# Rows 4 and 5 of a Fourier mix: their own products in place of mirrored reads of the products of rows 1 and 2

## The chip, the cores and the metric

The kernel runs on one core of one Trainium2 chip. A core has TensorE (PE) for matrix products, VectorE (DVE), ScalarE (ACT) and GpSimd (POOL) for elementwise work, and SyncE (SP), which here only issues transfers. ACT and POOL issue transfers as well, in line with their other instructions. Each engine works through its own list in order, and semaphores order the engines against each other and against the 16 DMA engines. The metric is device time of one execution in microseconds (us), as the median of three runs; the profile is of one further recorded look at one execution, with its own time.

## The reference

The input is q, k, v of shape (4 batches, 8 heads, 768 positions, 64). First comes attention with ALiBi slopes, in which a position sees the 96 latest positions and the first 8; then a Fourier mix and a two-layer product with a residual:

```
x = attention(q, k, v)                       # per batch 768 x 512
X = np.fft.fft(np.fft.fft(x, axis=1), axis=2)
u = x + np.real(X)
un = (u - mean(u)) / sqrt(var(u) + 1e-6)     # over the 512 columns
out = u + relu(un @ w_ch1) @ w_ch2           # 512 x 2048, 2048 x 512
```

The real part of a 2-D transform of real numbers is symmetric: its value at (position s, column d) is the value at (768 - s, 512 - d), both taken modulo the size.

## The kernel before

**Tiling.** A position is written as s = 6m + r, with m from 0 to 127 on the partitions and r from 0 to 5, the "row" of the title. A column is d = 4n + rd. The transform is split so that a short sum over tiles is made on VectorE and the rest are matmuls. Each batch b passes through these steps: loads and casts of q, k, v (`load`, L353; `cast_qk`, L407; `cast_v`, L475); transposes (`trans`, L499); scores, exponential and mask (`score`, L545); the product with v (`av`, L672), which gives X[b]; `bounce` (L727), which writes x to a DRAM buffer `xd` in plain order and reads it back as rows; the folds (`fold_s`, `fold_d`), which are sums and differences on VectorE; `y_unit` (L910), the transform over positions, 14 blocks (rs, rd) in eight PSUM half banks, copied to the tile `zy`; `u_unit` (L988), the transform over columns, 16 matmuls of 128 columns for one pair of rows, into PSUM tile `pu`; `u_rows` (L1011), which adds x (tile `xr`) on VectorE and takes the row sums; `un` (L1046), the normalised rows; `nt_unit` (L1072), their transposes; and per pair of rows ("chunk" c = 3b + pair, 12 in all) the two products `ph_unit` (L1119, 8 PSUM tiles of 8 matmuls) and `pg_unit` (L1142, for each of two rows 16 matmuls of 512 columns). The last row of the last chunk is made in two halves of 256 columns (`pg_last`, L1184). The sum of product and u goes to one of two buffers `ob` and from there to `out`.

**Rows 4 and 5 before.** Three pairs make a batch, `PAIRS = ((1, 2), (5, 4), (0, 3))`. Only two of them have products of their own. By the symmetry row 5 is row 1 with m and d reversed, and row 4 is row 2. So `u_unit(b, 0)` calls `u_rows` twice on the same `pu`: for rows 1 and 2, and again for rows 5 and 4, reading `pu` with both column indices reversed (L1026). The partition index m can't be reversed by VectorE, so for this pair everything beside the product is held with m reversed: `bounce` reads x's rows 4 and 5 from `xd` in reversed m into a second DRAM buffer `xe` (L750), and reads that back to `xr1` (L754); the output goes to a DRAM buffer `oe` (L1172), and from there in reversed m to `out` (`back`, L1179). Two two-column copies (L1021, L1034) handle the column that maps to itself.

```
eng.dma_start(XE[0], rows[::-1, 4:6].rearrange("m a d -> a m d"))            # L750
o = out[b].rearrange("(m r) d -> m r d", r=6)[::-1, rs, :]                   # L1178
eng.dma_start(o.rearrange("m (h d) -> h m d", h=2), cell[1].rearrange(...))  # L1179
```

**The order of the work.** The instruction order is not written by hand. A planner (`Plan`, L18) keeps a time for each engine, with a written cost per step, and lets the step that can start first go next; among PE streams (`MIX`: transform, `ATT`: attention, `PH`, `PG`: the two products) the order of the list breaks ties. What it gives is fixed in the program: on the chip every engine follows this order, and an instruction whose input is late holds up all that stand behind it on its engine. A transfer also waits for the earlier one that used the same of eight completion semaphores, whichever of SP and ACT issued it. `bounce` issues its transfers from SP for batch 0 and from ACT for batches 1 to 3. Stores of `out` and `oe` go out on ACT for chunks 0 to 5 and on SP for chunks 6 to 11 (L1167). Two one-row transfers on SP ("hold", L1289, L1290) keep the loads of batch 2 back until a part of w2 has landed, and those of batch 3 until `xr` of batch 1 has.

Of the kernel before, what the change touches and what calls it, by code (L numbers as in the profile page):

```python
# [14 lines left out]
P = 128  # L15


class Plan:  # L18
# [67 lines left out]
    def emit(self, place):  # L86
        ready, (_, ways, needs, after, outs, uses, ring, lat, dma, then, _) = self.ready.pop(place)
        ends = [max(self.t[w[0]], r) + w[1] for w, r in zip(ways, ready)]
        i = int(np.argmin(ends))
        eng, _, fn = ways[i]  # L90
        fn()
        end = self.t[eng] = ends[i]
        if dma:
            q = "DMA2" if eng == "ACT" or outs and outs[0][0] in ("xw", "xr", "xrb") else "DMA"
            end = self.t[q] = max(self.t[q], end) + dma
        for o in outs:
            self.tok[o] = end + lat if dma else (end + lat, eng)
        for u in uses:
            self.used(u, end + lat)
        if ring is not None:  # L100
            self.rings[ring].append(end)
        if then is not None:
            then(end + lat)
        self.promote()
# [71 lines left out]
def kernel(  # L176
# [91 lines left out]
    def bank(tag, name, dtype=FP32):  # L268
# [7 lines left out]
        return early["late"].tile([P, 512 if dtype == FP32 else 1024], dtype, tag=tag, name=name, bufs=RING[tag])  # L276


    NBUF = {"hT": 3, "vs": 2, "qk": 2, "qs": 3, "qkT": 4, "er": 2, "eg": 1, "x": 1, "xr0": 1, "xr1": 1, "xr2": 1, "zy": 1, "eA": 1,
# [207 lines left out]
    pl.users(("CD",), 4 * HP + 4 + 3 * NP + sum(len(ys) // 2 for ys in YG))  # L487
# [239 lines left out]
    def bounce(b):  # L727
# [14 lines left out]
        XE = {}  # L742

        def rd():
            rows = XD[b].rearrange("(m r) d -> m r d", r=6)
            XR[b] = [buf(f"xr{i}", b, [P, 2, DP if i == 1 else Dm], FP16, 1) for i in range(3)]
            XE[0] = dr.tile([2, P, Dm], FP16, tag="xe", name=f"xe_{b}", bufs=2)
            eng.dma_start(XR[b][0], rows[:, 1:3])

            eng.dma_start(XE[0], rows[::-1, 4:6].rearrange("m a d -> a m d"))  # L750
            eng.dma_start(XR[b][2], rows[:, 0:4:3])
        pl.later([(on, 1.35, rd)], [("xw", b, 0), ("xw", b, 1)] + free("xr0", b) + free("xr1", b) + free("xr2", b), 0.0,
                 [("xr", b)], lat=2.0 if b else 0.6, dma=2.2, then=lambda t: pl.tok.__setitem__(("xri", b), pl.t[on]))
        pl.later([(on, 0.5, lambda: eng.dma_start(XR[b][1][:, :, 0:Dm], XE[0].rearrange("a p d -> p a d")))], [("xr", b)], 0.0,  # L754
                 [("xrb", b)], lat=2.0, dma=0.7)
# [76 lines left out]
    def IW(b, n):  # L832

        return (0, 1, 4, 6)[b] + n
# [75 lines left out]
    def y_unit(b, g, ts=None):  # L910
        def run(start, ring):
# [27 lines left out]
            def cp(on, lo, hi):  # L939
                if ("y", b) not in T:  # L940
                    T[("y", b)] = buf("zy", 2 * b + 1, [P, 8, 2, 2, P], FP16, 3)
# [16 lines left out]
        MIX.append(([("w", b, 2 if b == 0 and g > 1 else 0 if g in (0, 3) else 1), ("c", "t1" if b else "t0")], ("ph",) if b == 1 else ("C", "D") if b == 0 and g > 1 else BANKS(b), run))  # L958
# [13 lines left out]

    def ysrc(rs, rd):
        if (rs, rd) in POS:
            return rs, rd, False
        return rs, 4 - rd, True

    PAIRS = ((1, 2), (5, 4), (0, 3))  # L980
    DP = Dm + 2
# [6 lines left out]
    def u_unit(b, pr):  # L988
        src = {(a, rd): ysrc(rs, rd) for a, rs in enumerate(PAIRS[pr]) for rd in range(4)}
        needs = [("y", b, r2, d2) + (("r",) if m else ()) for r2, d2, m in src.values()]  # L990

        def run(start, ring):
            pu = bank(ring, f"pu_{NP * b + pr}")
# [7 lines left out]
            pl.used(("free", "zy", 2 * b + 1), e)  # L1001
            if pr:
                for _ in range(2):
                    pl.used(("free", "rev0", b), e)
                u_rows(NP * b + pr, pu, e, ring)
            else:
                u_rows(NP * b, pu, e, None)
                u_rows(NP * b + 1, pu, e, ring)
        MIX.append((needs + ([("unT", NP * b + 1 - b)] if b < 2 and pr else []), ("xx",), run))

    def u_rows(c, pu, e, ring):  # L1011

        b, pr = divmod(c, NP)

        def add(rows):
            if c not in UT:
                UT[c] = buf("u", HP + c, [P, 2, DP], FP32, 2)
                MV[c] = wk.tile([P, 2, 4], FP32, tag="sm", name=f"sm_{c}", bufs=6)
            u, sm, xr = UT[c], MV[c], XR[b][pr]
            if pr == 1:  # L1020
                V.tensor_copy(xr[:, :, Dm:Dm + 1], xr[:, :, 0:1])  # L1021
            for a in rows:
                if pr == 1:

                    o, xx = u[:, a, 1:Dm + 1], xr[:, 1 - a, 1:Dm + 1]
                    i = pu[:, a].rearrange("p (r n) -> p r n", r=4)[:, ::-1, ::-1].rearrange("p r n -> p n r")  # L1026
                else:
                    o, xx = u[:, a, 0:Dm], xr[:, a]
                    i = pu[:, a].rearrange("p (r n) -> p n r", r=4)
                V.scalar_tensor_tensor(o.rearrange("p (n r) -> p n r", r=4), i, 1.0,  # L1030
                                       xx.rearrange("p (n r) -> p n r", r=4),
                                       op0=ALU.mult, op1=ALU.add, accum_out=sm[:, a, 0:1])
            if pr == 1:
                V.tensor_copy(u[:, :, 0:1], u[:, :, Dm:Dm + 1])  # L1034
            V.tensor_scalar_mul(sm[:, rows[0]:rows[-1] + 1, 1], sm[:, rows[0]:rows[-1] + 1, 0], -SC / Dm)  # L1035

        cuts = [(0,), (1,)] if c in (0, NP) else [(0, 1)]
        for rows in cuts:
            last = rows is cuts[-1]
            pl.later([("DVE", len(rows) * dve(512) + 0.15 + 0.15 * (pr == 1), lambda rows=rows: add(rows))],  # L1040
                     [("xrb" if pr == 1 else "xr", b)] + free("u", HP + c) + ([("unT", 0)] if c in (1, 2) else [])
                     + ([("u", c, 0)] if rows == (1,) else [("u", c - 1, 1)] if pr == 1 else []), e, [("u", c, a) for a in rows],
                     [("free", f"xr{pr}", b)] if last else [], ring=ring if last else None)
        cell = {}

        def un(on, a):  # L1046

            if 0 not in cell:
                cell[0] = T[("un", c)] = buf("un", 1 + c, [P, 2, Dm], FP16, 4 if c in (0, NP) else 3)
            m = MV[c][:, a, 1:2]  # L1050
            if on == "ACT":
                A(cell[0][:, a], UT[c][:, a, 0:Dm], AF.Identity, m, SC)  # L1052
            else:
                V.tensor_scalar(cell[0][:, a], UT[c][:, a, 0:Dm], SC, m, op0=ALU.mult, op1=ALU.add)
        for a in range(2):
            pl.later([("ACT", 0.81, lambda a=a: un("ACT", a)), ("DVE", 0.56, lambda a=a: un("DVE", a))],
                     [("u", c, a)] + free("un", 1 + c), 0.0, [("un", c, a)])

        def square(a):
            x = cell[0][:, a]  # L1060
            A(x, x, AF.Square, accum_out=MV[c][:, a, 2:3])  # L1061
        for a in range(2):
            pl.later([("ACT", 0.85, lambda a=a: square(a))],
                     [("unT", c)], 0.0, [("ss", c, a)], [("free", "un", 1 + c)], rank=3)

        def rstd():
            r = MV[c][:, :, 3]
            nc.gpsimd.tensor_scalar(r, MV[c][:, :, 2], 1.0 / Dm, SC * SC * 1e-6, op0=ALU.mult, op1=ALU.add)  # L1068
            nc.gpsimd.tensor_tensor(r, r, mhalf, op=ALU.pow)
        pl.later([("POOL", 1.0, rstd)], [("ss", c, 0), ("ss", c, 1)], 0.0, [("rstd", c)], rank=2)  # L1070

    def nt_unit(b, pr, rows=(0, 1)):  # L1072
# [12 lines left out]
        def run(start, ring):  # L1085
            if rows[0] == 0:
                PTU[0] = bank(ring, f"ptu_{c}", FP16)
                PTU[1] = ring
                if ring == "ph":
                    PTU[0] = PTU[0].rearrange("p (a m) -> p a m", a=2)  # L1090
# [11 lines left out]
            def cp(on):  # L1102
# [6 lines left out]
                else:  # L1109
# [3 lines left out]
                     [("unT", c, a) for a in rows] + ([("unT", c)] if rows[-1] else []), ring=PTU[1] if rows[-1] else None)  # L1113
        MIX.append(([("un", c, a) for a in rows] + [("unT0", c)][:rows[0]], (("ph",) if c == NP else ("xx",)) if rows[0] == 0 else None, run))
# [27 lines left out]
    def pg_unit(c, t, part):  # L1142
# [4 lines left out]
        def run(start, ring):  # L1147
# [13 lines left out]
            def add():  # L1161
                cell[0] = buf("ob", i, [P, Dm], FP32, 1)
                V.scalar_tensor_tensor(cell[0], pg, MV[c][:, t, 3:4], UT[c][:, t, 0:Dm],  # L1163
# [3 lines left out]
            eng = nc.scalar if c < 6 else nc.sync  # L1167

            def st():
                if pr == 1:  # L1170
                    cell[1] = dr.tile([P, Dm], FP32, tag="oe", name=f"oe_{c}_{t}", bufs=4)
                    eng.dma_start(cell[1], cell[0])  # L1172
                else:
                    eng.dma_start(out[b].rearrange("(m r) d -> m r d", r=6)[:, rs, :], cell[0])
            pl.later([("ACT" if c < 6 else "SP", 0.45, st)], [("ob", i)], 0.0, [("st", i)], [("free", "ob", i)], lat=1.6, dma=0.7)

            def back():
                o = out[b].rearrange("(m r) d -> m r d", r=6)[::-1, rs, :]  # L1178
                eng.dma_start(o.rearrange("m (h d) -> h m d", h=2), cell[1].rearrange("m (h d) -> h m d", h=2))  # L1179
# [209 lines left out]
```

## Time and profile before

| | |
|---|---|
| time, three runs | 317.89 us median (315.81 to 319.12) |
| the profiled execution | 317.89 us, of which the span from first to last instruction is 316.1 us |
| mean granted TensorE clock | 0.932 |
| PE, PE weight loads, DVE, ACT, POOL busy | 264.3, 174.4, 176.3, 134.6, 65.5 us |
| HBM read, written | 35.62 MB, 12.58 MB |

The profile gives the busy time of each engine; for each instruction its line, its operation, its output and input tiles, its start and length, and in square brackets how long its engine had stood idle before it and what ended the wait; the chain of waits that ended last; and for each transfer the time from issue to landing. "SPq" and "ACTq" are transfers issued by SP and ACT; "PEclk" is the granted clock in tenths. A wait is put down to the releaser that came last by the profile's records, which need not be the one the program names.

### The profile page before, as it was taken

How to read it: one execution, taken by the hardware profiler on the slowest of the kernel's cores; microseconds unless marked ns; L12 is line 12 of the kernel's file. 1: busy time of each engine (PE TensorE's matmuls, PEld its weight loads, DVE VectorE, ACT ScalarE, POOL GpSimd, SP SyncE). 2: the span in 40 equal slices, each digit the busy share in tenths (PEclk: the TensorE clock that was granted, in tenths of full speed). 3: DMA queues.
4: the chain of work that ended last, by engine and by line, in shares of the span. 5: the costliest groups of instructions: out<-in, count | busy, mean ns of one | idle time of the engine just before them, and what ended most of it. 6: DMA issues, size and time to landing. Idle time of an engine off the chain costs nothing.

```text
span 316.1 us, 5868 instructions
## 1 busy us (share of the span) xinstructions
PE 264.3 (84%) x2346; PEld 174.4 (55%) x2346; DVE 176.3 (56%) x369; ACT 134.6 (43%) x226; POOL 65.5 (21%) x119
## 2 busy tenths in 40 slices
PE   8888961899999862789999589989999999999930
PEld 3446730677765330557786354558677577675520
DVE  4759731594878931568899347668967414201200
ACT  3786330567553320568823125584335353341000
POOL 1666023148301520204542000002100110100000
PEclk9999995599999967799999969999999999999995
DMA  8999598655999926964989224211631323101221
GB/s 225 295 322 218 135 226 225 159 139 87 193 235 278 310 93 144 207 190 109 168 133 182 96 69 94 75 34 36 150 120 41 109 68 86 65 33 68 80 79 40
DMA packets 87142, 44.38 MB, mean 140 GB/s; under 512 B 45900, under 2 KB 83276, under 8 KB 86988
## 3 DMA queue, kind: packets, MB, share of 16 engines
q1 hardware_dynamic: 72494, 30.12, 39.2%
q10 hardware_dynamic: 10398, 9.70, 10.5%
q0 software_dynamic: 4224, 4.19, 8.2%
q8 instruction: 18, 0.29, 0.4%
q14 instruction: 8, 0.07, 0.1%
HBM read 35.62 MB, written 12.58 MB: 152 GB/s over the span
## 4 chain that ended last, share of the span: by engine, by line
PE 41%; DMA 24%; DVE 11%; SPq 8%; issue 6%; POOL 5%; ACT 2%; ACTq 1%; POOLq 0%; DVEq 0%
PE ph L1129 16%; PE pg L1152 14%; DMA xe<-xd 6%; DMA oe<-ob 5%; SPq L371 4%; SPq L405 3%; DMA vs<-in_v_dram 3%; DVE x L718 3%; DMA w<-in_moe_w_ch_dram 3%; DMA out_dram<-ob 2%; DMA qs<-in_q_dram 2%; PE sc L569 2%; PE pu L998 2%; DVE u L1030 2%; POOL qk L423 2%
## 5 line engine op out<-in xcount | busy, mean ns | idle before, releaser
L1129 PE MATMUL ph<-unT,w 128*128 128x256 f16 x768 | 96.4, 276 | 7.5 <-DVE hT L1136 7.2
L1152 PE MATMUL pg<-w,hT 128*128 128x512 f16 x368 | 88.2, 386 | 0.0
L1129 PEld LDWEIGHTS <-w 128*128 128x128 f16 x768 | 72.8, 99 | 25.8 <-issue 13.8
L1135 ACT ACTIVATE hT<-ph 128x512 f16<-128x512 f32 x62 | 36.8, 597 | 55.0 <-PE ph L1129 46.7
L1152 PEld LDWEIGHTS <-hT 128*128 128x128 f16 x368 | 35.3, 99 | 37.5 <-issue 3.5
L592 ACT ACTIVATE er<-sc 128x992 f16<-128x992 f32 (+2 forms) x42 | 37.8, 923 | 17.2 <-PE sc L569 9.1
L1163 DVE SCALAR_TENSOR_TENSOR ob<-pg,sm,u 128x512 f32<-128x512 f32 x23 | 17.2, 748 | 39.1 <-PE pg L1152 33.4
L607 DVE TENSOR_TENSOR ex<-er,mk 128x992 f16<-128x992 f16 (+2 forms) x42 | 27.7, 674 | 15.1 <-ACT er L592 15.0
L1136 DVE TENSOR_SCALAR hT<-ph 128x512 f16<-128x512 f32 x34 | 23.3, 688 | 18.3 <-PE ph L1129 17.9
L1068 POOL TENSOR_SCALAR sm<-sm 128x2 f32<-128x2 f32 x12 | 2.3, 193 | 105.7 <-ACT un L1061 105.5
L945 ACT ACTIVATE zy<-py 128x512 f16<-128x512 f32 x17 | 9.8, 596 | 31.6 <-DMA vs<-in_v_dram 11.4
L423 POOL CAST qk<-qs 128x768 f16<-128x768 f32 x21 | 18.1, 873 | 15.0 <-DMA qs<-in_q_dram 5.7
L512 POOL COPY kG<-qkT 64x8 f16<-64x8 f16 x32 | 9.2, 287 | 53.5 <-DVE qkT L540 27.4
L569 PE MATMUL sc<-qkT 64*128 64x256 f16 (+1 forms) x192 | 17.0, 266 | 3.8 <-DVE u L1030 2.5
L531 PE MATMUL pt<-ident,qk 128*128 128x128 f16 x144 | 12.4, 245 | 8.9 <-ACT er L592 4.5
L1030 DVE SCALAR_TENSOR_TENSOR u<-pu,xr 128x512 f32<-128x512 f32 x24 | 15.8, 688 | 3.6 <-PE pu L998 3.3
L718 DVE TENSOR_TENSOR x<-pav,rc 128x512 f16<-128x512 f32 (+1 forms) x27 | 17.1, 632 | 0.9
L1061 ACT ACTIVATE un<-un 128x512 f16<-128x512 f16 x24 | 14.8, 621 | 5.7 <-DMA unT<-un 2.4
L1052 ACT ACTIVATE un<-u,sm 128x512 f16<-128x512 f32 x12 | 8.4, 718 | 20.0 <-DVE sm L1035 19.9
L947 DVE CAST zy<-py 128x512 f16<-128x512 f32 x11 | 7.4, 688 | 15.9 <-ACT zy L945 9.7
L698 PE MATMUL pav<-v,ex 128*128 128x65 f16 x352 | 16.3, 193 | 0.0
L698 PEld LDWEIGHTS <-ex 128*128 128x128 f16 x352 | 15.1, 97 | 2.0 <-DVE rc L717 0.4
(112 smaller groups left out, 288.0 us busy)
## 6 DMA issues: line engine op xcount, KB each, us to landing
vs<-in_v_dram SPq DMA_DIRECT2D x24, 192.0 KB, 5.2
w<-in_moe_w_ch_dram POOLq DMA_DIRECT2D x8, 512.0 KB, 9.3
qs<-in_q_dram SPq DMA_DIRECT2D x9, 384.0 KB, 7.4
qs<-in_k_dram SPq DMA_DIRECT2D x9, 384.0 KB, 5.7
xd<-x ACTq DMA_DIRECT2D x12, 192.0 KB, 5.6
out_dram<-ob ACTq DMA_DIRECT2D x8, 256.0 KB, 2.0
out_dram<-ob SPq DMA_DIRECT2D x7, 256.0 KB, 2.1
u<-in_v_dram SPq DMA_DIRECT2D x4, 384.0 KB, 6.0
```

The source lines that it names most:

```text
L423: nc.gpsimd.tensor_copy(d, s)
L569: nc.tensor.matmul(pa[:, s, c0:c0 + cw], TT[n][lo:lo + 64, 1, i * P:(i + 1) * P], TT[n][lo:lo + 64, 0, i * P:i * P + cw], start=(not inps) ...
L592: A(mine(), cut(pa), AF.Exp, 0.0, 0.125)
L607: VT(o, mine(), m, op=ALU.mult)
L698: nc.tensor.matmul(po[:, jj, hh * 65:(hh + 1) * 65], lhsT, v16[b % 2][:, i, h, 0:65], start=(jp == 0 and a == 0), stop=(a == len(ops) - 1) ...
L718: VT(X[b][:, 2 * jp:2 * jp + 2, first * Dh:(first + nh) * Dh].rearrange("p j (h d) -> p j h d", d=Dh), pv[:, :, :, 0:Dh], rc.to_broadcast( ...
L1030: V.scalar_tensor_tensor(o.rearrange("p (n r) -> p n r", r=4), i, 1.0, xx.rearrange("p (n r) -> p n r", r=4), op0=ALU.mult, op1=ALU.add, a ...
L1129: nc.tensor.matmul(ph[:, a * CH:(a + 1) * CH], w1[:, d, jb * P:(jb + 1) * P], UNT[c][:, d, :], start=(d == 0), stop=(d == ND - 1))
L1135: pl.later([("ACT", act(512), lambda: A(dst, ph, AF.Relu)), ("DVE", dve(512), lambda: V.tensor_scalar_max(dst, ph, 0.0))], [], e, [("h", c ...
L1136: ("DVE", dve(512), lambda: V.tensor_scalar_max(dst, ph, 0.0))],
L1152: nc.tensor.matmul(pg, HT[c][:, jb, t * P:(t + 1) * P], w2[:, jb, :], start=(jb == 0), stop=(jb == NJ - 1))
L1163: V.scalar_tensor_tensor(cell[0], pg, MV[c][:, t, 3:4], UT[c][:, t, 0:Dm], op0=ALU.mult, op1=ALU.add)
```

## The change

Rows 4 and 5 get products of their own, and nothing is reversed in DRAM.

- The pairs are `((1, 2), (0, 3), (4, 5))`. `u_unit` is called for each of them, 16 matmuls each time, and its VectorE part is the same for all three.
- Rows 4 and 5 take the blocks of rows 2 and 1 with both signs turned (`ysrc`): blocks `(6 - rs, 4 - rd)`, reversed along m. So `mirror` gains four steps `rn` per batch, each of which copies two blocks (128x512 elements in all) of `zy` in reversed order into a new tile in the ring `ww`, on ACT or POOL in batch 0 and on ACT or DVE after it.
- `bounce` reads x in two transfers of three rows each (128 x 1536 elements) in place of three transfers and the read back from `xe`; `xe` and `oe` are gone, and all rows are stored to `out` straight from `ob`.
- In batch 0 the first chunk's `u_unit` is placed after the block group (2, 0), and the third chunk's waits for the second tile of the first product.

```diff
-            XR[b] = [buf(f"xr{i}", b, [P, 2, DP if i == 1 else Dm], FP16, 1) for i in range(3)]
-            XE[0] = dr.tile([2, P, Dm], FP16, tag="xe", name=f"xe_{b}", bufs=2)
-            eng.dma_start(XR[b][0], rows[:, 1:3])
-            eng.dma_start(XE[0], rows[::-1, 4:6].rearrange("m a d -> a m d"))
-            eng.dma_start(XR[b][2], rows[:, 0:4:3])
-        pl.later([(on, 0.5, lambda: eng.dma_start(XR[b][1][:, :, 0:Dm], XE[0].rearrange("a p d -> p a d")))], [("xr", b)], 0.0,
-                 [("xrb", b)], lat=2.0, dma=0.7)
+            XR[b] = [buf(f"xr{i}", b, [P, 3, Dm], FP16, (3, 3)[i]) for i in range(2)]
+            for i in range(2):
+                eng.dma_start(XR[b][i], XD[b].rearrange("(m r) d -> m r d", r=6)[:, 3 * i:3 * i + 3])
...
+        def rn(n, on):
+            if n == 0:
+                T[("rev", b)] = buf("ww", IW(b, NA(b) + 1), [P, 4, 2, 2, P], FP16, 1)
+            rev = T[("rev", b)]
+            d, y = rev[:, n], T[("y", b)][:, n, :, :, ::-1]
+            if on == "ACT":
+                A(d, y, AF.Copy)
+            else:
+                (V if on == "DVE" else nc.gpsimd).tensor_copy(d, y)
...
-        return rs, 4 - rd, True
-    PAIRS = ((1, 2), (5, 4), (0, 3))
+        return (6 - rs) % 6, (4 - rd) % 4, True
+    PAIRS = ((1, 2), (0, 3), (4, 5))
...
-                u_rows(NP * b, pu, e, None)
-                u_rows(NP * b + 1, pu, e, ring)
+            def add(rows):
...
+                    V.scalar_tensor_tensor(u[:, a].rearrange("p (n r) -> p n r", r=4),
+                                           pu[:, a].rearrange("p (r n) -> p n r", r=4), 1.0,
+                                           XR[b][(r0, r1)[a] // 3][:, (r0, r1)[a] % 3].rearrange("p (n r) -> p n r", r=4),
+                                           op0=ALU.mult, op1=ALU.add, accum_out=sm[:, a, 0:1])
...
-                if pr == 1:
-                    cell[1] = dr.tile([P, Dm], FP32, tag="oe", name=f"oe_{c}_{t}", bufs=4)
-                    eng.dma_start(cell[1], cell[0])
-                else:
-                    eng.dma_start(out[b].rearrange("(m r) d -> m r d", r=6)[:, rs, :], cell[0])
-            def back():
-                o = out[b].rearrange("(m r) d -> m r d", r=6)[::-1, rs, :]
-                eng.dma_start(o.rearrange("m (h d) -> h m d", h=2), cell[1].rearrange("m (h d) -> h m d", h=2))
+                (nc.scalar if c < 6 else nc.sync).dma_start(out[b].rearrange("(m r) d -> m r d", r=6)[:, rs, :], cell[0])
...
-            mirror(b)
-            for rows in ((0,), (1,)) if b < 2 else ((0, 1),):
-                nt_unit(b, 0, rows)
-            nt_unit(b, 1)
-            u_unit(b, 2)
-            nt_unit(b, 2)
+            mirror(b)
+            if b:
+                u_unit(b, 0)
+            u_unit(b, 1)
+            for rows in ((0,), (1,)) if b < 2 else ((0, 1),):
+                nt_unit(b, 0, rows)
+            u_unit(b, 2)
+            nt_unit(b, 1)
+            nt_unit(b, 2)
```

The planner orders both kernels anew from these steps, so instructions of other parts move as well.

## The prediction

> **What bounds the kernel now.** I read the span in slices first, then the chain of waits backwards from its end, then PE's own waits. In the slices (40 of 7.9 us) the rows are busy tenths of PE and the granted clock:
>
> ```profile
> PE   8888961899999862789999589989999999999930
> ...
> PEclk9999995599999967799999969999999999999995
> ```
>
> PE has work in nearly all slices; the holes are slice 6 (47 to 55 us), 14 and 15 (111 to 126), 22 (174 to 182) and the end. In the second row the clock falls beside each hole. So PE's stream bounds the span, plus what stands in these four places, and I price the change by place.
>
> **The end.** The chain of waits, with start, length and what, ends so:
>
> ```profile
> 295.98 0.76 DVE ob L1163
> ...
> 296.76 7.09 DMA oe<-ob
> ...
> 303.86 0.61 SPq L1179
> ...
> 304.57 7.83 DMA out_dram<-ob
> ...
> 312.51 0.48 DVE ob L1201
> ```
>
> SP issues in order. Its read of `oe` (L1179) waits until `oe` has landed, the direct stores queue behind it, and only when they land is there an `ob` for the last add (L1201). The last matmuls run from 299.23 for 3.66 us and end at 302.89: PE is done 9.6 us before that add starts.
>
> **The other holes.** PE's rows after each hole, with the releaser in brackets:
>
> ```profile
> 56.80 3.57 PE L1129 MATMUL ph<-unT,w 128*128 128x256 f16 x16 [6.42 <-DVE hT L1136]
> 183.29 0.37 PE L928 MATMUL py<-t,ww 128*128 128x256 f16 x1 [4.93 <-ACT zy L945]
> ```
>
> and what held up the releaser, on DVE and on ACT:
>
> ```profile
> 54.36 0.17 DVE L1021 COPY xr<-xr 128x2 f16<-128x2 f16 x1 [11.32 <-DMA xr<-xe]
> 112.61 1.00 ACT L592 ACTIVATE er<-sc 128x992 f16<-128x992 f32 x1 [7.43 <-DMA qs<-in_k_dram]
> 126.03 0.32 ACTq L1172 DMA_DIRECT2D oe<-ob  x1
> 126.40 0.60 ACT L945 ACTIVATE zy<-py 128x512 f16<-128x512 f32 x1 [11.45 <-DMA vs<-in_v_dram]
> 181.65 0.38 ACTq L754 DMA_DIRECT2D xr<-xe  x1
> 182.15 1.08 ACT L945 ACTIVATE zy<-py 128x512 f16<-128x512 f32 x2 [5.52 <-DMA xe<-xd]
> ```
>
> Each is an engine standing in order at something of the reversed rows: DVE at the two-column copy of `xr`, ACT at the issue of L754, and ACT at the store to `oe` (L1172), which waits for a completion semaphore that a load of v of a later batch holds. All three go.
>
> **Part by part.** Base: the profiled execution, 317.9 us, span 316.1 and 1.8 around it; it equals the median of the three runs.
>
> *T, the tail.* All stores are direct. The last add can start some 0.1 us after the last matmul, at 303.0 in place of 312.5: **−9.5**. Does another wait stand there? The two `ob` are filled by the adds at 295.98 and 299.49 (0.75 each); direct stores on SP land 2.1 us after issue (median of seven), so the buffers are free at about 299 and 302.5, before 303.0. The cover is only 0.5 us, so −8.5 to −9.5.
>
> *P, products.* Four more groups of 16 matmuls. The chain has such a group at 0.89 us (189.86) and, at the lower clock, 1.24 (129.34): 4 x 0.89 = **+3.6**; from 2.7 (the one of batch 0 falls in a hole) to 5.0.
>
> *M, reversed copies.* 16 of 512 elements. ACT's L945 copies as many in 0.60 us; 16 x 0.6 = 9.6 us, on ACT (43% busy) and DVE (56%), that is 2.4 per batch. The work that hides them is `ph` and `pg`, which PE has ready in the steady stretches; only the copy ahead of the third product can show: **+1**; 0 to +4, the latter if no such work stands ready in two batches (2 x 2.4, rounded down).
>
> *A, 47 to 57 us.* DVE goes on without the 11.32 us; the `hT` copies queued behind L1021 free PE's `ph` buffers. PE has matmuls to do from about 50 us, after the transposes at 49.55. The wait of 6.42 goes, and the 16 matmuls after it, 3.57 in place of 1.75 at full clock (chain, 249.94), lose 1.8: 8.2 at most. What is late next is POOL's cast of qk, which already held PE for 3.04 us there, and the loads of w2, which nothing here speeds up. **−5** (0 to −8).
>
> *B, 109 to 135 us.* Here ACT stops twice: for `xd` to land, then for 3.2 us in issuing L751 (112.5), and again for 11.45 at the `oe` store. PE waits 4.46 (to 113.66), 6.76 (to 127.05) and 2.50 (to 135.23), and runs the matmuls between at half clock, 3.3 and 1.35 longer: 18.4 in all. After, the exponential stands ahead of the wait for `xd`, and the stretch has no store to `oe`; but ACT still waits for `xd` itself, and a store with a shared semaphore can still be late. **−14** (−6, the sum of the first wait and little more, to −18.4).
>
> *C, 174 to 188 us.* ACT's wait for `xe` to land (10.75 us in the chain, from 170.88) goes with L750 and L754, so the `zy` copies no longer stand behind it. PE's 4.93 and 2.3 of half clock (14 `py` in 2.94 where 1.5 would do, 4 `pg` in 1.70 for 0.86) make 7.2; **−6** (−3 to −7.3).
>
> *D, small.* Waits of 0.78, 0.76 (205 to 208, ACT at L1179) and 1.04 (237, ACT at L754) of the same kind: **−2** (0 to −2.6).
>
> *N, new waits.* x's rows now come in two transfers of three rows in place of three of two, so the second pair (rows 0, 3) needs both of them. In the holes removed, PE's work moves ahead of loads that don't. No row shows these waits. Below: nothing, or a gain of 2, a guess at what the loads win when some 3 MB (4 x 0.26 of `xe`, 8 x 0.26 of `oe`) are no longer moved beside them; above: 10, the size of the wait for L754 in one batch. I take **+4**, about 1.3 per batch from 1 on, nearest to the small waits of 0.8 to 2.5 in PE's rows.
>
> Sum: −9.5 + 3.6 + 1 − 5 − 14 − 6 − 2 + 4 = −27.9, **290.0 us**. All good ends together give 317.9 − 9.5 + 2.7 − 8 − 18.4 − 7.3 − 2.6 − 2 = 272.8; all bad ones 317.9 − 8.5 + 5 + 4 − 6 − 3 + 10 = 319.4.
>
> **Two rules weighed.** The trace has the transfers of the tail at 7.09 (`oe<-ob`) and 7.83 us (`out_dram<-ob`, with the queue ahead of it). The Trainium skill, "DMA: Bandwidth & Descriptors", section "Anatomy of one DMA — SWDGE (gpsimd) path", fits 2.0 us plus the bytes over 436 GB/s: an estimate of 2.6 us for 256 KB, which speaks against T: by it the way from 296.76 through `oe`, L1179 (0.6) and the stores would be over at about 302.6, before PE is done, T would be 0 and the sum 299.5. The direct stores agree with the rule (2.1), the way through DRAM does not, and the rows decide. On the clock: the rows show half speed after each hole of 4.5 us and more, none after those of about 1. The skill's "TensorE: Matmul & The Clock Gate" puts the half clock after an idle window of some 3.4 us; by it, a hole of B that shrinks to 4 us and no further would keep its 3.3 us.
>
> **Rivals.**
>
> 1. *The holes refill.* ACT's wait for `xd` and POOL's casts are still there, and the loads of later batches come when they come: A and B then give nothing. For it: the second releaser at 112.61 is a load of k, and POOL's casts hold PE beside A. Against: ACT's 11.45 ends at L1172, an instruction that is gone, and DVE's at L1021, likewise. It would give 290.0 + 5 + 14 = 309. In part it is likely, which fills the stretch from 297 to 309.
>
> 2. *The holes close wholly*, the copies hide, and fewer transfers meet the loads: 273 to 279.
>
> 3. *Only the tail less the products*, with C and D lost as well to a wait for `xr` rows 3 to 5 in each batch: 317.9 − 9.5 + 3.6 + 1 = 313.0.
>
> 4. *Slower: direct stores on ACT stand at a shared semaphore.* Chunks 0 to 5 store from ACT, and each store waits for the transfer that used its semaphore last. Where that is a load held back, ACT stops with everything behind it: the exponentials, the `zy` and `hT` copies. The price is in the trace, 11.45 us once. For it: the planner does not know these semaphores, and ACT now issues as many stores as before. Against: today one of ACT's 12 stores (8 at L1174, 4 at L1172) pays this, and where I followed the order of the new kernel no held load is the one waited for. It decides from three such stops, 3 x 11.45 = 34 against 27.9: 324.
>
> That the change does not do what it says is excluded by the order of the new kernel's instructions, which holds the third group of products and no transfer through `xe` or `oe`.
>
> **Chances.** Forecast with its own spread (279 to 297) 0.60; rival 1 (297 to 310) 0.22; rival 2 0.06; rival 3 (310 to 314.7) 0.05; within 1% 0.03, the bad ends together; rival 4 0.04. A measurement of this kernel tells about 1% from no change, as its runs lie from 315.8 to 319.1. So faster 0.93, same 0.03, slower 0.04. The range, 279 to 309, leaves out 0.06 below and about 0.13 above.
>
> **What the profile after should show.** T: the last add directly behind the last matmul, and the end some 3.6 us after it, as now (312.51 to 316.1). P: 64 more matmuls at the line of `pu`, 0.89 us per 16. M: 16 reversed copies of about 0.6 us. A: no wait of 11 us on DVE near 50 us. B and C: no ACT wait above 5 us ahead of a `zy` copy, clock tenths of 9 in the slices around 115 to 130 and 180 to 190. N: any new wait of PE above 2 us is mine to name. The forecast is wrong if ACT or DVE stands as long at `xr<-xd`, at `xd`, or at a store as it now does at `xe` and `oe`, or if PE's rows name POOL's casts in place of ACT.

## The result and the profile after

The change makes the kernel faster: 273.1 us (median of four runs, 272.08 to 274.13) against 316.85 us (315.67 to 319.12); the ratio is 0.861, with a 95% interval from 0.855 to 0.868. The forecast was 290.0 with a range from 279 to 309. The direction and the mechanism were right; the gain was 44 us in place of 28, and the time lies below the range.

The profiled execution after took 272.08 us, with a span of 270.1. Its page, busy tenths and granted clock in 40 slices of 6.75 us:

```profile
PE   7789898999999979899999799999999999999994
...
PEclk9999999999999999999999999999999999999999
```

The four holes of the kernel before are gone, and with them every slice at a lower clock. The mean clock is 1.00 where it was 0.932.

The end of the span after, by the timeline (start, length, what, and in brackets the wait and what ended it):

```profile
262.80 3.66 PE L1174 MATMUL pg<-w,hT 128*128 128x256 f16 x32
...
266.50 0.48 DVE L1182 SCALAR_TENSOR_TENSOR ob<-pg,sm,u 128x256 f32<-128x256 f32 x1 [1.26 <-PE pg L1174]
```

The last add now waits for PE alone, and starts 0.04 us after the last matmul. From there to the end of the span it is 3.6 us, as before.

PE's waits after (in all, how often, longest), those between the start-up and the end that the prediction's "new waits" stood for:

```profile
PE pu L1006 <- ACT zy L937: 1.4, 1, 1.4
...
PE sc L569 <- ACT er L592: 1.0, 1, 1.0
PE pt L531 <- POOL qk L423: 0.9, 2, 0.5
```

None is above 2 us. No wait of PE names a reversed copy (L971, L973). One of 0.29 us on VectorE, at 150.59, does stand ahead of the `zy` copies that end the wait of 1.4 us, so up to 0.3 of that wait may be owed to it.

**Where the 46.0 us of the span went.** These are figures of the two profiled executions. PE's idle time fell from 51.8 us (316.1 less 264.3 busy) to 14.4 (270.1 less 255.7), by 37.4. Its busy time fell by 8.6, although it has more to do: the products `pu` take 14.8 us in place of 11.1, 3.7 more, so all other matmuls, which are the same in number and shape, take 12.3 us less. Most of that is the clock: in the four stretches of the kernel before at a granted clock of 0.5 (48.0 to 61.6 us, 112.8 to 119.7, 123.1 to 129.9 and 181.1 to 187.9), PE is busy for 5.6, 6.0, 2.9 and 4.6 us, 19.1 in all, and at full clock this work would take some 9.6, an estimate. Of the other 2.7, 1.0 lies in the first 10 us, at the same clock in both (8.64 against 7.63 busy); the rest is not assigned. One group of the transform over positions, before and then after:

```profile
L928 PE MATMUL py<-t,ww 128*128 128x256 f16 x36 | 9.4, 313 | 6.0 <-ACT zy L945 4.9 <-DVE zy L947 1.0
```

```profile
L920 PE MATMUL py<-t,ww 128*128 128x256 f16 x36 | 7.8, 273 | 0.0
```

The same 36 matmuls have a mean of 273 ns in place of 313, and no wait. Place by place, with the idle time of PE from the windows of both kernels:

| step | forecast, us | measured, us |
|---|---|---|
| T, end of the span | −9.5 | −9.6 (13.2 to 3.6) |
| P, products | +3.6 | +3.7 busy time |
| M, reversed copies | +1 | at most 0.3 seen in PE's waits |
| A, 46 to 57 us | −5 | −9.5 of idle time |
| B, 109 to 135 us | −14 | −13.7 of idle time |
| C, 178 to 188 us | −6 | −4.9 of idle time |
| D, small waits | −2 | −2.6 of idle time |
| half clock beside A, B, C | in A, B, C | −9.6 of busy time (2.8, 4.4 and 2.3) |
| other busy time | 0 | −2.7 |
| N, new waits | +4 | +3.7 (2.3 at 90 to 110 us, 1.4 at 153) |
| other places | 0 | −0.8 |
| sum | −27.9 | −46.0 |

The 2.3 us lie in the stretch that B has become, and the 1.4 in that of C, so N may as well be read as what is left of B and C.

### The profile page after: what moved, and what is told of

It reads as the page before. It is cut to its first block, busy times and chain, and to the rows that moved or that the text cites. A ratio compares the mean times of both kernels' runs of the same rounds, so it can differ in the third digit from the quotient of the medians.

```text
span 270.1 us, 5988 instructions
## 1 busy us (share of the span) xinstructions
PE 255.7 (95%) x2410; PEld 173.0 (64%) x2410; DVE 177.9 (66%) x364; ACT 139.0 (51%) x238; POOL 66.8 (25%) x120
## 4 chain that ended last, share of the span: by engine, by line
PE 69%; DMA 11%; DVE 6%; SPq 6%; POOL 4%; issue 3%; ACT 1%; POOLq 0%; DVEq 0%
PE ph L1122 27%; PE pg L1145 23%; DMA qs<-in_q_dram 4%; PE pu L1006 4%; DMA w<-in_moe_w_ch_dram 3%; PE sc L569 3%; DMA vs<-in_v_dram 3%; SPq L371 3%; SPq L405 3%; PE pav L698 2%; PE py L916 2%; DVE x L718 2%; PE py L920 2%; PE pg L1174 1%; PE py L923 1%
## 5 line engine op out<-in xcount | busy, mean ns | idle before, releaser
L1122 PE MATMUL ph<-unT,w 128*128 128x256 f16 x768 | 94.4, 273 | 0.2 <-DVE unT L1103 0.2
L1145 PE MATMUL pg<-w,hT 128*128 128x512 f16 x368 | 86.3, 379 | 0.0
L1128 ACT ACTIVATE hT<-ph 128x512 f16<-128x512 f32 x58 | 34.6, 597 | 50.5 <-PE ph L1122 50.2
L1129 DVE TENSOR_SCALAR hT<-ph 128x512 f16<-128x512 f32 x38 | 26.1, 688 | 12.8 <-PE ph L1122 12.6
L607 DVE TENSOR_TENSOR ex<-er,mk 128x992 f16<-128x992 f16 (+2 forms) x42 | 29.6, 721 | 2.7 <-ACT er L592 2.6
L569 PEld LDWEIGHTS <-qkT 64*128 64x128 f16 x192 | 6.4, 94 | 13.0 <-issue 10.2
L479 POOL CAST v<-vs 128x768 f16<-128x768 f32 x12 | 10.5, 879 | 15.1 <-DMA vs<-in_v_dram 15.0
L330 PE MATMUL fill<-eg 128*128 128x512 f16 x46 | 12.6, 419 | 1.4 <-DVE eg L1207 1.2
L512 POOL COPY kG<-qkT 64x8 f16<-64x8 f16 x32 | 8.4, 263 | 21.0 <-DVE qkT L540 10.4
```

What stands on the lines that cost most here:

```text
L569: nc.tensor.matmul(pa[:, s, c0:c0 + cw], TT[n][lo:lo + 64, 1, i * P:(i + 1) * P], TT[n][lo:lo + 64, 0, i * P:i * P + cw], start=(not inps) ...
L607: VT(o, mine(), m, op=ALU.mult)
L1122: nc.tensor.matmul(ph[:, a * CH:(a + 1) * CH], w1[:, d, jb * P:(jb + 1) * P], UNT[c][:, d, :], start=(d == 0), stop=(d == ND - 1))
L1128: pl.later([("ACT", act(512), lambda: A(dst, ph, AF.Relu)), ("DVE", dve(512), lambda: V.tensor_scalar_max(dst, ph, 0.0))], [], e, [("h", c ...
L1129: ("DVE", dve(512), lambda: V.tensor_scalar_max(dst, ph, 0.0))],
L1145: nc.tensor.matmul(pg, HT[c][:, jb, t * P:(t + 1) * P], w2[:, jb, :], start=(jb == 0), stop=(jb == NJ - 1))
```

## The experiments

Two theories were put against each other. The first: every hole has its own releaser among the transfers of reversed rows, holes add up, and the transfers themselves, not only the waits for them, make the holes. The second: the holes have other waits behind them and refill, so that part of the gain is owed to the new order of the work. In all edits but one (a_order) PE, DVE and the computing instructions of ACT and POOL keep their order; only transfers are changed, taken away or issued elsewhere, and in a_prod2 matmuls are added. The kernel before ran beside each: its runs lay from 314.2 to 322.2 us, with medians of 317.6 to 319.1. The kernel after did not run beside them; its 273.1 us are from the rounds in which the kernel before had 316.85, so a difference from it is sure to some 2 us only.

**The stores alone (b_oe).**

```diff
-                if pr == 1:
-                    cell[1] = dr.tile([P, Dm], FP32, tag="oe", name=f"oe_{c}_{t}", bufs=4)
-                    eng.dma_start(cell[1], cell[0])
-                else:
-                    eng.dma_start(out[b].rearrange("(m r) d -> m r d", r=6)[:, rs, :], cell[0])
+                eng.dma_start(out[b].rearrange("(m r) d -> m r d", r=6)[:, rs, :], cell[0])
...
-                eng.dma_start(o.rearrange("m (h d) -> h m d", h=2), cell[1].rearrange("m (h d) -> h m d", h=2))
+                pass
```

> The kernel before, with rows 5 and 4 stored straight from ob to out; nothing is read back from oe (left out: the reversal of m of these rows' output). Each engine's order is as before, less the removed issues. Theory (each hole has its own releaser, and holes add up): the tail goes, 9.5 us, the 11.45 us stop of ACT at the store to oe in batch 1 with 10 us of PE's holes, and 1.5 of the wait at 205 us: about 296 us. Rival (holes refill, because other waits stand behind them): only the tail goes, about 307 us.

Measured: 295.66 us (294.65 to 296.34), 22.0 less than the kernel before (ratio 0.931, from 0.925 to 0.937). The theory had 296.

**The read of x alone (b_xe).**

```diff
-            XE[0] = dr.tile([2, P, Dm], FP16, tag="xe", name=f"xe_{b}", bufs=2)
...
-            eng.dma_start(XE[0], rows[::-1, 4:6].rearrange("m a d -> a m d"))
+            eng.dma_start(XR[b][1][:, :, 0:Dm], rows[:, 4:6])
...
-        pl.later([(on, 0.5, lambda: eng.dma_start(XR[b][1][:, :, 0:Dm], XE[0].rearrange("a p d -> p a d")))], [("xr", b)], 0.0,
+        pl.later([(on, 0.5, lambda: None)], [("xr", b)], 0.0,
```

> The kernel before, with x's rows 4 and 5 read straight from xd into xr1, in plain m; xe is gone (left out: the reversal of m of x for these rows). Theory: DVE no longer stands 11.3 us at the two-column copy, which takes the whole hole from 46 to 57 us, 9.5 of idle time and some 2.5 of half clock; the hole at 178 to 188 goes, 7.2; 1.0 at 237; and in batch 1 the rows behind xe land earlier, which lets the held loads and the ACT stop end some 6 us sooner: about 291 us. Rival (refill): only the hole at 178 goes, since casts on POOL keep the one at 46 and the store to oe the one of batch 1: about 309 us.

Measured: 293.28 us (292.81 to 295.96), 24.4 less (ratio 0.925, from 0.918 to 0.932); the theory had 291. The whole stretch from 46 to 55 us is filled: PE's busy time there is 9.00 of 9 us. In batch 1 the stop of ACT at the store to `oe` is still there, by the timeline of this run:

```profile
108.94 0.34 ACTq L1172 DMA_DIRECT2D oe<-ob  x1
109.33 0.60 ACT L945 ACTIVATE zy<-py 128x512 f16<-128x512 f32 x1 [11.03 <-DMA vs<-in_v_dram]
```

So this part of B belongs to the stores, as b_oe says from the other side, and the rest of B to the read of x.

**Both (b_oe_xe).** The two edits together.

> The kernel before, with both edits: no reversed row goes through DRAM, and still two products per batch (left out: the reversal of m of x and of the output for rows 4 and 5). Theory: the sum of all holes, and no third product: the time of the kernel after less 3.6 for the products and less its new waits of 3.7, about 266 us. Rival (the new order of the first chunk's work earns a part of the gain): well above the kernel after, some 280 us.

Measured: 270.60 us (270.00 to 273.39), 47.0 less than the kernel before. The two single edits give 22.0 + 24.4 = 46.4, each sure to some 2 us, so within that they add up, and holes do not refill. The old order of the work, without the round trips, earns all of it; the kernel after is this one plus a third product, 270.6 + 3.6 = 274.2, and has 273.1. The theory's 266 took off the new waits as well, and was too low: this kernel has such waits too, 2.9 us of PE's time for `er` alone.

**The order of batch 0 undone (a_order).**

```diff
-                    if (b, g, t) == (0, 2, 0):
+                    if (b, g, t) == (0, 1, 1):
                         u_unit(b, 0)
...
-        MIX.append((needs + ([("h", 0, 1)] if c == 2 else []), BANKS(b) if pr < 1 else ("xx",), run))
+        MIX.append((needs + [], BANKS(b) if pr < 1 else ("xx",), run))
```

> The kernel after, with the first chunk's u of batch 0 placed after the block group (1, 1), as it was before the change, and without the wait of the third chunk's product for the second tile of the first; the planner orders the rest anew. Theory (the gain is the end of the waits for reversed rows, not the order): within 2 us of the kernel after, 272 to 275 us. Rival (the new order fills the stretch from 46 to 57 us): 278 us or more.

Measured: 275.27 us (274.58 to 277.17), 2.2 above the kernel after, or 0.8%, at the edge of what can be told (1.4, if each is taken by its ratio to the kernel before beside it). It lies just above the theory's range and well below the rival's 278: the new order of batch 0 is worth some 2 us.

**The third product twice (a_prod2).**

```diff
-            for (a, rd), (r2, d2, mir) in src.items():
+            for (a, rd), (r2, d2, mir) in list(src.items()) * (2 if pr == 2 else 1):
```

> The kernel after, with the 16 matmuls of the third pair issued twice, the second time over the first, in all four batches: 64 more matmuls of 128 columns, as the change had added 64. Theory (they stand on PE's continuous stream): 4 x 0.89 = 3.6 us more, 276.7 us. Rival (they fall into holes of PE): 273 us.

Measured: 276.41 us (275.27 to 277.76), 3.3 more than the kernel after (2.7 by the ratios). That is near the theory's 3.6, and the rival's 273 is not reached: the products stand on PE's stream, and little or nothing hides them.

**One transfer that nobody reads (a_xe).** The kernel after, with the reversed transfer put back between its two reads of x:

```diff
             for i in range(2):
                 eng.dma_start(XR[b][i], XD[b].rearrange("(m r) d -> m r d", r=6)[:, 3 * i:3 * i + 3])
+                if i == 0: eng.dma_start(dr.tile([2, P, Dm], FP16, tag="xe", name=f"xe_{b}", bufs=2), XD[b].rearrange("(m r) d -> m r d", r=6)[::-1, 4:6].rearrange("m a d -> a m d"))
```

> The kernel after, with the transfer of rows 4 and 5 from xd to xe put back between the two reads of x, in all four batches; nobody reads xe and nobody waits for it. All else is as in the kernel after. Theory (the transfer is slow, and the read behind it in the queue lands late, so the second read of x, and with it the u of the second pair and the held loads, come some 5 us later in each batch): 278 to 285 us. Rival (only waits of an engine for the reversed rows cost time, not their transfers): 273 to 275 us.

Measured: 296.52 us (294.65 to 299.04). A transfer of 0.26 MB per batch, whose data nobody uses, costs 23.4 us, more than the theory's 5 to 12. PE's timeline in the stretch of A, first in the kernel before, then in this one:

```profile
46.00 0.51 PE L531 MATMUL pt<-ident,qk 128*128 128x128 f16 x6 [0.91 <-POOL qk L423]
49.55 0.82 PE L531 MATMUL pt<-ident,qk 128*128 128x128 f16 x6 [3.04 <-POOL qk L423]
```

```profile
47.99 0.82 PE L531 MATMUL pt<-ident,qk 128*128 128x128 f16 x6 [2.49 <-POOL qk L423]
51.33 0.82 PE L531 MATMUL pt<-ident,qk 128*128 128x128 f16 x6 [2.52 <-POOL qk L423]
```

These are the waits for POOL's casts of the kernel before, back again, though DVE waits for no reversed row. Why POOL is late stands in its own rows. The cast of q in this stretch, in the kernel before, the kernel after and this one:

```profile
45.13 0.82 POOL L423 CAST qk<-qs 128x768 f16<-128x768 f32 x1 [4.61 <-DMA qs<-in_q_dram]
```

```profile
42.32 0.82 POOL L423 CAST qk<-qs 128x768 f16<-128x768 f32 x1 [1.19 <-DMA qs<-in_q_dram]
```

```profile
47.12 0.82 POOL L423 CAST qk<-qs 128x768 f16<-128x768 f32 x1 [5.84 <-DMA qs<-in_q_dram]
```

The load of q, issued on SP behind the reversed transfer, lands 3 to 5 us later. What the DMA engines moved from 37 to 40 us shows the same (the last two columns are their busy share and GB/s), for the kernel before, after, and this one:

```profile
37.00:40.00 3.00, 2.55 (x31) 2.15 (x29) 1.51 (x5) 1.24 (x4) 1.08 (x4) 1.00 0.62 175
```

```profile
37.00:40.00 3.00, 3.00 (x36) 2.58 (x35) 1.52 (x3) 2.23 (x5) 1.04 (x4) 1.00 1.02 336
```

```profile
37.00:40.00 3.00, 3.00 (x37) 2.68 (x35) 1.36 (x3) 2.23 (x5) 0.88 (x3) 1.00 0.58 176
```

In batch 1 ACT stands 4.33 us in issuing the second read of x, where it took 1.52 at most after, and the exponential behind it makes PE wait:

```profile
107.22 0.97 ACT L592 ACTIVATE er<-sc 128x960 f16<-128x960 f32 x1 [8.75 <-DMA qs<-in_k_dram]
108.24 0.50 PE L569 MATMUL sc<-qkT 64*128 64x256 f16 x4 [6.44 <-ACT er L592]
```

In batch 2 that read is released only when a transpose by DMA lands, of which it needs no data; I read this as a shared completion semaphore. All of ACT waits with it:

```profile
165.40 1.08 ACT L1129 ACTIVATE hT<-ph 128x512 f16<-128x512 f32 x2 [10.56 <-DMA qkT<-qk]
```

PE waits 8.53 us there. The four waits of PE make 20.0 us; the granted clock is 0.5 beside them, which adds to it.

**The same transfer in another shape (a_xe16).** Bytes, place and queue are as in a_xe; the rows stand in plain order, so that the outermost size is 128:

```diff
-                if i == 0: eng.dma_start(dr.tile([2, P, Dm], FP16, tag="xe", name=f"xe_{b}", bufs=2), XD[b].rearrange("(m r) d -> m r d", r=6)[::-1, 4:6].rearrange("m a d -> a m d"))
+                if i == 0: eng.dma_start(dr.tile([P, 2, Dm], FP16, tag="xe", name=f"xe_{b}", bufs=2), XD[b].rearrange("(m r) d -> m r d", r=6)[:, 4:6])
```

> The kernel after, with an idle transfer of rows 4 and 5 from xd to xe between the two reads of x, as in the run that had it reversed, and in the same place of the same queue, but in plain m with an outermost size of 128 in place of 2 (256 in the reversed form, of which one side has an outermost size of 2). Same bytes; nobody reads xe. Theory (the shape is what made the reversed one cost 23 us: it is served slowly, and all that lands behind it is late): 273 to 276 us. Rival (one more transfer, with its issue and the completion semaphore that later loads share, is what costs): 285 us or more.

Measured: 275.14 us (273.51 to 276.03), 2.0 above the kernel after (0.7 by the ratios). So of the 23.4 us some 21 are owed to the shape, and 2 at most to one more transfer with its issue and its semaphore. The shape means three things here: the outermost size, the reversal, and the size of the pieces (a_xe moves 1,032 packets more than the kernel after, a_xe16 577). The next edit keeps the reversal and makes the pieces smaller still.

**The round trips on more engines (b_k4).** The kernel before, with the outermost size of its slow transfers raised from 2 to 4; the read back of `xe` follows the new layout:

```diff
-            XE[0] = dr.tile([2, P, Dm], FP16, tag="xe", name=f"xe_{b}", bufs=2)
+            XE[0] = dr.tile([P, 2 * Dm], FP16, tag="xe", name=f"xe_{b}", bufs=2)
...
-            eng.dma_start(XE[0], rows[::-1, 4:6].rearrange("m a d -> a m d"))
+            eng.dma_start(XE[0].rearrange("m (g d) -> g m d", g=4), rows[::-1, 4:6].rearrange("m a (h d) -> (a h) m d", h=2))
...
-        pl.later([(on, 0.5, lambda: eng.dma_start(XR[b][1][:, :, 0:Dm], XE[0].rearrange("a p d -> p a d")))], [("xr", b)], 0.0,
+        pl.later([(on, 0.5, lambda: eng.dma_start(XR[b][1][:, :, 0:Dm], XE[0].rearrange("p (a d) -> p a d", a=2)))], [("xr", b)], 0.0,
...
-                eng.dma_start(o.rearrange("m (h d) -> h m d", h=2), cell[1].rearrange("m (h d) -> h m d", h=2))
+                eng.dma_start(o.rearrange("m (h d) -> h m d", h=4), cell[1].rearrange("m (h d) -> h m d", h=4))
```

> The kernel before, with the two transfers that had an outermost size of 2 (xe from xd, and out from oe) cut into four columns blocks of 512 B pieces, so an outermost size of 4 in place of 2. Same order, same waits, same bytes. Theory (these transfers run on as few DMA engines as their outermost size, and what lands late behind them makes the holes): they take half as long, some 4 us in place of 8; each of the holes at 46, 109, 178 and at the end shrinks by about 3 to 4 us: 300 to 306 us. Rival (the holes are the count of steps through DRAM and their fixed latencies): 315 to 318 us.

Measured: 303.90 us (301.54 to 305.78), 15.2 less than the kernel before beside it (319.08; ratio 0.954, from 0.947 to 0.962). All work and all waits of the round trips are still there. The end of its chain of waits:

```profile
286.19 4.69 DMA oe<-ob
...
291.61 6.11 DMA out_dram<-ob
```

These were 7.09 and 7.83. Both are stores whose own shape the edit leaves as it was; each stands behind a read back of `oe` (L1179), issued on SP just ahead of it, and that one has the new shape. In batch 2 `xe`, by the chains of the kernel before and of this one, takes

```profile
170.88 10.75 DMA xe<-xd
```

```profile
167.69 7.60 DMA xe<-xd
```

The hole at 46 us did not shrink, against the expectation:

```profile
PE ph L1129 <- DVE hT L1136: 11.3, 2, 10.6
```

```profile
DVE xr L1021 <- DMA xr<-xe: 10.9, 1, 10.9
```

The waits for POOL's casts are gone there, but DVE stands as long as before: SP issues the read back of `xe` at 48.97 us, behind its loads of q, k and v, and at 49.51 in the kernel before. So in b_k4 this hole is set by the place of the read back in SP's order, and another shape alone does not close it.

While a read back of `oe` runs alone, the kernel before shows, at its end (the last two columns again):

```profile
301.00:303.00 2.00, 1.89 (x18) 1.45 (x15) 0.00 (x0) 0.00 (x0) 0.00 (x0) 1.00 0.14 49
```

A share of 0.14 of 16 engines is 2.2 of them. In b_k4 such a transfer, alone from 248 to 249 us, has a share of 0.26, which is 4.2 engines, and moves 78 GB/s. The Trainium skill, "DMA: Bandwidth & Descriptors", section "Why a DMA increments its semaphore by 16 and not by 1", says that a transfer runs on the largest number of engines up to 16 that divides the slowest sizes of both sides. For the transfers to `xe` and from `oe` that is 2, for b_k4's 4, and for a_xe16's 16. The shares of 2.2 and 4.2 engines agree with it; a_xe16's never runs alone, so that no share shows its 16.

**ACT's stop (b_pool_oe, b_act).** ACT's 11.45 us of batch 1 were read as a wait for a completion semaphore. First only the stores to `oe` of chunks below 6 went to POOL:

```diff
-                    eng.dma_start(cell[1], cell[0])
+                    (nc.gpsimd if c < 6 else eng).dma_start(cell[1], cell[0])
```

> The kernel before, with the stores to oe of batches 0 and 1 issued from POOL in place of ACT, all else as it is. Theory (ACT's 11.45 us are a wait for a completion semaphore shared with a held load, and POOL's transfers have others): the wait of PE of 6.76 us in batch 1, the 1.35 of half clock behind it and the 2.5 after go, about 307 us. Rival (what ACT waits for is late anyway): no change, 317 us.

Measured: 317.97 us (ratio 1.003, from 0.998 to 1.007). No change, and the expectation failed. ACT's rows show where it stands now:

```profile
128.04 0.38 ACTq L754 DMA_DIRECT2D xr<-xe  x1
128.47 0.81 ACT L592 ACTIVATE er<-sc 128x768 f16<-128x768 f32 x1 [8.54 <-DMA vs<-in_v_dram]
```

The next transfer on ACT is released, by the records, by the same held loads. So that one, and the reads back of `oe` for chunks below 6, were moved to POOL too:

```diff
-        pl.later([(on, 0.5, lambda: eng.dma_start(XR[b][1][:, :, 0:Dm], XE[0].rearrange("a p d -> p a d")))], [("xr", b)], 0.0,
+        pl.later([(on, 0.5, lambda: (nc.gpsimd if b == 1 else eng).dma_start(XR[b][1][:, :, 0:Dm], XE[0].rearrange("a p d -> p a d")))], [("xr", b)], 0.0,
...
-                eng.dma_start(o.rearrange("m (h d) -> h m d", h=2), cell[1].rearrange("m (h d) -> h m d", h=2))
+                (nc.gpsimd if c < 6 else eng).dma_start(o.rearrange("m (h d) -> h m d", h=2), cell[1].rearrange("m (h d) -> h m d", h=2))
```

> The kernel before, with all of ACT's issues of batches 0 and 1 that wait for a held load's completion semaphore moved to POOL: the stores to oe, the reads back of oe, and the read of xe in batch 1. The first of the three alone changed nothing, since ACT then stood at the next, the read of xe. Theory (the stop of 11.45 us on ACT is these waits): PE's 6.76, 1.35 and 2.5 us go, some 10 us, less what POOL's own casts lose while POOL stands at the transfers: 307 to 312 us. Rival (POOL stands as long as ACT did, and its casts are as much in PE's way): 316 us or more.

Measured: 309.80 us (308.57 to 310.62), 9.3 less than the kernel before beside it (319.05; ratio 0.974, from 0.968 to 0.980), within the theory's range. POOL now stands in ACT's place:

```profile
125.07 0.73 POOL L754 DMA_DIRECT2D xr<-xe  x1 [11.72 <-DMA xe<-xd]
```

Between 105 and 140 us PE now waits 3.9 us for `er`, 3.3 for `unT` and 0.5 for `qkT`, and no longer for the `zy` copy. So it is ACT's standing at these issues, several in a row, that cost PE its time. What held each of them is not the same. For the store to `oe` it is the load of v, since in b_xe, without `xe`, the stop is as long. For the read of `xe` it need not be the semaphore: on POOL it is released by `xe` itself, at 125.07, 16.5 us after the issue of that transfer on ACT (108.54). On ACT, in b_pool_oe, it went at 128.04, so the semaphore may have added some 3 us; the runs don't part the two.

**A version meant to be faster (a_rdpool).** The kernel after, with x's reads of batches 1 to 3 issued from POOL, so that ACT does not stand 3.36 us before an exponential at 94 us:

```diff
-                eng.dma_start(XR[b][i], XD[b].rearrange("(m r) d -> m r d", r=6)[:, 3 * i:3 * i + 3])
+                (nc.gpsimd if b else eng).dma_start(XR[b][i], XD[b].rearrange("(m r) d -> m r d", r=6)[:, 3 * i:3 * i + 3])
```

> The kernel after, with the two reads of x in batches 1 to 3 issued from POOL in place of ACT, all else in the same order. Theory: ACT no longer stands 3.36 us at 94 us, ahead of an exponential that PE waits for, so up to 2.3 us of the new waits go: 271 to 273 us. Rival (POOL stands there with its casts of q, k and v, which PE needs as much): 273 to 277 us.

Measured: 272.53 us (six runs, 271.44 to 273.80), 0.6 below the kernel after, which is no difference that can be told. The time lies in the theory's range, but the trace shows the rival's mechanism: PE's wait of 1.0 us for `er` goes, and its waits for POOL's casts of qk grow from 0.9 to 2.1 us.

What the 16 reversed copies cost by themselves was not measured. In the trace after they are 7 on ACT at 0.63 us, 8 on DVE at 0.29 and 1 on POOL at 0.61.

## Why the prediction was wrong

The steps T, P and D held. M was too dear by some 0.7 to 1, as far as PE's waits show. N has the right size, 3.7 for +4, by luck: of its two reasons, waits for x's rows did not come, as nothing waits for `xr` in the trace after, and PE's work moving ahead of loads fits only the 0.9 us at POOL's casts; the other waits name `er`, `unT` and `zy`.

The step that failed is the pricing of the holes, −25 for A, B and C. Idle time and half clock together, A gave −12.3 us for −5, B −18.1 for −14 and C −7.2 for −6. The full ends that the prediction named for B and C, 18.4 and 7.3, are what came. For A even the full end, 8.2, was too small: of its 9.5 us of idle time it counted 6.42 and left out the 3.04 at POOL's cast. I then took 9.3 us off the full ends of A to D (36.3). The discount and the 3.04 make 12.3 of the 18.1 us by which the sum was off. Half clock that the prediction left out, 9.6 for the 8.75 that it counted, makes 0.9, and 2.7 is busy time that these holes don't explain.

The step behind the discount reads, for A: "What is late next is POOL's cast of qk, which already held PE for 3.04 us there, and the loads of w2, which nothing here speeds up", and for B that ACT still waits for `xd` itself. Both took the waits next to the holes for independent of the reversed rows. They were not: a_xe brings back the waits for POOL's casts and, in batch 1, 6.44 us of PE's wait for an exponential, with one transfer that nobody reads; a_xe16, in another shape, has 0.3 us of waits for the casts and 3.05 for the exponential. The prediction had named a gain for this under N ("a guess at what the loads win") and priced it at 2 us, as one end of a range; the runs put the cost of the slow shape at 21 us in the kernel after.

Of the rivals, the second, that the holes close wholly (273 to 279, chance 0.06), is what happened. The first, that they refill to 309, had 0.22; b_oe_xe speaks against it directly, as both edits together give the sum of each. The fourth, direct stores on ACT at a shared semaphore, came about only in small. In the trace after, ACT stands once at the issue of the reads of x until a direct store has landed, and PE waits 1.0 us for the exponential behind it:

```profile
94.38 0.97 ACT L592 ACTIVATE er<-sc 128x960 f16<-128x960 f32 x1 [3.36 <-DMA out_dram<-ob]
```

In the weighing of the two rules, the first, by which T would be 0, was rightly set aside: the measured T is 9.6. The prediction takes it from the section on the gpsimd path, and these transfers were issued by SP; what the estimate left out is the queue. The store to `oe` of 7.09 us stood behind a read back issued 1.4 us ahead of it, and with that one cut for 4 engines the same two steps took 4.69 and 6.11 us.

On the clock, other runs bear on the length of the idle window that the second rule names. The granted clock fell to 0.5 at shorter waits of PE than 3.4 us: at 2.49 us in a_xe (47.99), 2.51 in b_oe_xe (97.98) and 3.05 in a_xe16 (98.36). It did not at 2.50 us in the kernel before (135.23). So a hole of B that shrank to 4 us could well have kept its half clock, and so could one of 2.5; the trace after has no wait above 1.4 us past the start, and no slice at a lower clock.

## What to carry to other kernels

A transfer that is slow by its shape costs more than the wait for its data: what was queued behind it landed late here, and engines that stand in order far from it showed the loss under other names. So before calling a neighbouring wait independent of the transfers that a change removes, see what was queued behind them; where the DMA engines' share is low while transfers are pending, count the whole hole and the half clock beside it, as came true here for B and C. A transfer can also be late by its place in the issuing engine's order, as the read back of `xe` was in b_k4, and then another shape does not help. And an engine may stand at several issues in a row; taking away the first such wait showed nothing here until the others were gone.

## What the runs showed of the hardware that was not expected

A DRAM-to-DRAM transfer of 0.26 MB per batch with an outermost size of 2 on one side, which nothing reads, made a kernel of 273.1 us take 296.5; the same bytes with an outermost size of 128, in plain order and larger pieces, made it 275.1. While it was pending in a_xe, from 158 to 160 us, the engines moved 48 GB/s. A store of 256 KB to `oe`, issued at 293.36 us in the kernel before with nothing slow just ahead of it, was followed by its read back 2.0 us later; the next one, issued at 296.76 behind that read back, took 7.1 us, the last one in b_xe 7.1 as well, and in b_k4 4.7.

Waits of PE of 2.5 us were followed by half the granted clock in two runs, a_xe and b_oe_xe, and not in the kernel before.
